# A gated mixer on one core: first block of w_in loaded in one piece, gate row third on ScalarE's queue, second half of block 0 used early

## The chip, the cores and the metric

One core of one Trainium2 chip. The metric is the device time of one execution in microseconds (us), the median over several executions, with the kernel before run in the same rounds. The text quotes means, ranges and the number of runs. All runs used for a comparison are fast, those without a lower clock and a longer time than their like. TensorE does not always get its full clock: in these traces it starts at half clock, at which equal matmuls start twice as far apart (107 against 56 ns for 128 columns), and goes to full clock some us later (at 3.54 to 9.90 us in the profiles below).

## The reference

The program mixes two branches of one input x (2048 rows of 512) with a gate per row:

```python
g = sigmoid((x * gate_w).sum(-1, keepdims=True))
a = A(x)     # linear attention, 32 heads of 16, softmax feature maps, then @ wo
b = B(x):    # z = gelu(x @ w_in), w_in is 512 x 1376
             # z1 = z[:, :688];  z2 = layernorm(z[:, 688:])
             # (z1 * (w_sp @ z2 + b_sp)) @ w_out
out = g * a + (1 - g) * b
```

All inputs are bf16. The change touches only the beginning of `x @ w_in[:, 688:]`: the second half of w_in, four blocks of 128 rows ("block 0" to "block 3"), multiplied with the first two tiles of x. The gate logits x @ gate_w ride along as a 689th column of the same weights.

## The kernel before: the parts that matter

The start of the kernel. HF is 344, FH is 688, P is 128, NDT is 4.

```python
    nc.gpsimd.dma_start(out=gaterow[0:NDT, :], in_=gate_w.rearrange("(dt p) -> dt p", p=P))
    ...
    nc.sync.dma_start(out=xs[:, 0, :], in_=x2[0:P, :])                             # x tile 0
    nc.scalar.dma_start(out=w_z2[:, 0, 0:HF], in_=w_in_v[:, 0, FH:FH + HF])        # block 0, first half
    nc.sync.dma_start(out=xs[:, 1, :], in_=x2[P:2 * P, :])                         # x tile 1
    load_z2w(nc.scalar, 1)                                                         # block 1
    load_z2w(nc.sync, 2)                                                           # block 2
    nc.scalar.dma_start(out=w_z2[:, 0, HF:FH], in_=w_in_v[:, 0, FH + HF:F])        # block 0, second half
    load_z2w(nc.sync, 3)                                                           # block 3
```

TensorE's program for the first two tiles. `one(tt, dt, j)` multiplies tile tt with block dt, columns of half j; `z_part` does a piece of the second half; `warm_up` multiplies constants, to keep TensorE busy until data arrive, and its result is thrown away; `x_T` transposes x through TensorE and copies it out of PSUM (VectorE or ScalarE); `gate_T` turns the gate row into four weight columns.

```python
        warm_up(6)                    # 6 matmuls of 512 columns
        warm_up(2, P)                 # 2 of 128 columns
        x_T(0, 0, 1, ...)             # needs x tile 0
        x_T(0, 1, NDT, ...)
        warm_up(3, P)
        one(0, 0, 0)                  # needs block 0, first half
        x_T(1, 0, 2, ...)
        x_T(1, 2, NDT, ...)
        one(0, 1, 0)                  # needs block 1
        warm_up(1, P)
        one(1, 0, 0)                  # needs the copy of x_T(1, ...)
        one(1, 1, 0)
        for tt in range(2):
            z_part(tt, 1, 0, HF, True)
        gate_T()
        for tt in range(2):
            z_part(tt, 0, 0, HF, False)   # needs block 0, second half
        one(0, 2, 0)
        ...
        for tt in range(2):
            one(tt, 3, 0)             # "row block 3 begins"
            one(tt, 3, 1)
            z2_out(tt, zps[tt])       # the first gelu on ScalarE
```

After that TensorE goes through the other tiles and the attention branch without a pause.

The softmax here doesn't subtract the row's maximum and nothing guards it: scores larger than these inputs give would overflow.

Of the kernel before, what the change touches and what calls it, by code (L numbers as in the profile page):

```python
# [14 lines left out]
P = 128  # L15
# [4 lines left out]
F = 1376  # L20
FH = 688
HF = FH // 2
NT = S // P
NDT = D // P
# [11 lines left out]
def kernel(  # L36
# [14 lines left out]
    nc = tc.nc  # L51
# [10 lines left out]
    xT = pers.tile([P, NDT, S], BF16, name="xT")  # L62
    w_z1 = early.tile([P, NDT, FH], BF16, name="w_z1")
    w_z2 = early.tile([P, NDT, WP], BF16, name="w_z2")
# [27 lines left out]
    gaterow = early.tile([P, P], BF16, name="gaterow")  # L92
# [3 lines left out]
    w_in_v = B_w_in.rearrange("(dt p) f -> p dt f", p=P)  # L96
# [7 lines left out]
        out=ramp[:, 0, :], data0=ones32[:, :], data1=zeros[:, :], initial=0.0,  # L104
# [4 lines left out]
    for q in range(4):  # L109
        qs = slice(32 * q, 32 * q + 32)  # L110
        nc.vector.tensor_tensor(
            out=ident[qs, qs], in0=ramp[qs, 0, :], in1=ramp[qs, 1, :], op=ALU.is_equal)
    nc.gpsimd.dma_start(out=gaterow[0:NDT, :], in_=gate_w.rearrange("(dt p) -> dt p", p=P))
    nc.gpsimd.memset(brow[:], 0.0)
    nc.gpsimd.memset(wphi[:], 0.0)
    def load_z2w(eng, dt):
        eng.dma_start(out=w_z2[:, dt, 0:FH], in_=w_in_v[:, dt, FH:F])  # L117

    nc.sync.dma_start(out=xs[:, 0, :], in_=x2[0:P, :])
    nc.scalar.dma_start(out=w_z2[:, 0, 0:HF], in_=w_in_v[:, 0, FH:FH + HF])  # L120
    nc.sync.dma_start(out=xs[:, 1, :], in_=x2[P:2 * P, :])
    load_z2w(nc.scalar, 1)
    load_z2w(nc.sync, 2)
    nc.scalar.dma_start(out=w_z2[:, 0, HF:FH], in_=w_in_v[:, 0, FH + HF:F])
    load_z2w(nc.sync, 3)
    scrap = early.tile([P, 1], BF16, name="scrap")
    nc.scalar.activation(
        out=scrap[:, :], in_=nc.const_aps.tensor(1.0, [P, 1], BF16), func=AF.Gelu_apprx_tanh)
# [5 lines left out]
    for h in range(2):  # L134
        nc.sync.dma_start(
            out=w_z1[:, 2 * h:2 * h + 2, :], in_=w_in_v[:, 2 * h:2 * h + 2, 0:FH])
    for i in range(4, 8):
        x_dma_T(i)
    for q in range(2, NCH):
        nc.sync.dma_start_transpose(  # L140
            out=xT[:, :, q * CH:(q + 1) * CH], in_=x2[q * CH:(q + 1) * CH, :]
        )
    nc.sync.dma_start(out=brow[0:NT, :], in_=B_b_sp.rearrange("(t p) -> t p", p=P))
    for qk in (1, 0):
        nc.sync.dma_start_transpose(
            out=wqkT[:, qk * NDT:(qk + 1) * NDT, :], in_=A_wqkv[:, qk * D:(qk + 1) * D])
# [4 lines left out]
    for h in range(2):  # L151
        nc.sync.dma_start(
            out=wv_sb[:, 2 * h:2 * h + 2, :],
            in_=A_wqkv[h * 2 * P:(h + 1) * 2 * P, 2 * D:3 * D].rearrange("(dt p) n -> p dt n", p=P),
        )
    for q in range(NCH):
        nc.sync.dma_start_transpose(
            out=wspT[:, :, q * CH:(q + 1) * CH], in_=B_w_sp[q * CH:(q + 1) * CH, :]
# [4 lines left out]
        out=mask4[:], in_=mask4[:], pattern=[[-32, NG]],  # L163
# [3 lines left out]
        out=mask4[:], in_=mask4[:], pattern=[[32, NG]],  # L167
# [3 lines left out]
        out=mask64[:, :, :], in_=mask4[:, :, None].to_broadcast([P, NG, DH]))  # L171
# [7 lines left out]
    def next_turn(kind, n):  # L179
        turn[kind] += 1  # L180
        return f"{kind}{(turn[kind] - 1) % n}"

    def zp_tile():
        return psA.tile([P, 2, CH], FP32, name="zp", tag=next_turn("zp", 3))

    def pq_tile(shape, dtype=FP32):
        return psF.tile(shape, dtype, name="pq", tag=next_turn("pq", 2))

    def z_one(zp, tt, wt, w, dt, j, first=0):
        n = HF if j == 0 else w - HF  # L190
        nc.tensor.matmul(  # L191
            zp[:, j, 0:n], lhsT=xT[:, dt, tt * P:(tt + 1) * P],
            rhs=wt[:, dt, j * HF:j * HF + n],
            start=(dt == first), stop=(dt == NDT - 1), skip_group_check=first > 0,
        )

    def z_mm(tt, wt, w):
        zp = zp_tile()
        for dt in range(NDT):
            for j in range(2):  # L200
                z_one(zp, tt, wt, w, dt, j)
        return zp

    def z2_out(tt, zp):
        z2v = z2all[:, tt, :].rearrange("p (j n) -> p j n", j=2)
        nc.scalar.activation(out=z2v, in_=zp[:, :, 0:HF], func=AF.Gelu_apprx_tanh)  # L206
        nc.vector.tensor_copy(out=glog[:, tt:tt + 1], in_=zp[:, 1, HF:HF + 1])
        for j in range(2):
            nc.vector.bn_stats(out=bn6[:, tt, j, :], in_=z2v[:, j, :])  # L209
        nc.vector.bn_aggr(out=mv[:, tt, :], in_=bn6[:, tt, :, :].rearrange("p j s -> p (j s)"))  # L210
# [4 lines left out]
    def z2_first_two():  # L215
        zps = [zp_tile() for _ in range(2)]
        tp1 = psA.tile([P, 2, P], BF16, name="tp1", tag=next_turn("zp", 3))
        turn["zp"] -= 1

        def warm_up(n, w=CH):  # L220
            for _ in range(n):
                nc.tensor.matmul(
                    zps[0][:, 1, 0:w], lhsT=nc.const_aps.tensor(1.0, [P, P], BF16),
                    rhs=nc.const_aps.tensor(1.0, [P, w], BF16), start=True, stop=True)

        def one(tt, dt, j):
            z_one(zps[tt], tt, w_z2, FH + 1, dt, j, first=j)

        def z_part(tt, dt, c0, c1, start):
            nc.tensor.matmul(  # L230
                zps[tt][:, 1, c0:c1], lhsT=xT[:, dt, tt * P:(tt + 1) * P],
                rhs=w_z2[:, dt, HF + c0:HF + c1], start=start, stop=False, skip_group_check=True)

        warm_up(6)
        warm_up(2, P)
        x_T(0, 0, 1, pq_tile([P, 1, P], BF16)[:, :, :])
        x_T(0, 1, NDT, pq_tile([P, 3, P], BF16)[:, :, :])
        warm_up(3, P)
        one(0, 0, 0)
        x_T(1, 0, 2, tp1[:, :, :])  # L240
        x_T(1, 2, NDT, pq_tile([P, 2, P], BF16)[:, :, :], on_act=True)
        one(0, 1, 0)
        warm_up(1, P)
        one(1, 0, 0)
        one(1, 1, 0)
        for tt in range(2):
            z_part(tt, 1, 0, HF, True)
        gate_T()
        for tt in range(2):
            z_part(tt, 0, 0, HF, False)  # L250
        one(0, 2, 0)
        one(1, 2, 0)
        for tt in range(2):
            one(tt, 2, 1)
            for dt in range(2):
                z_part(tt, dt, HF, HF + 1, False)
        for tt in range(2):
            one(tt, 3, 0)
            one(tt, 3, 1)
            z2_out(tt, zps[tt])  # L260
# [21 lines left out]
    def x_T(i, d0, d1, tp, on_act=False):  # L282
        for dt in range(d0, d1):
            nc.tensor.transpose(tp[:, dt - d0, :], xs[:, i, dt * P:(dt + 1) * P], ident[:, :])
        dst = xT[:, d0:d1, i * P:(i + 1) * P]
        if on_act:
            nc.scalar.copy(out=dst, in_=tp)
        else:
            with tc.high_priority():
                nc.vector.tensor_copy(out=dst, in_=tp)  # L290

    def gate_T():
        gt = pq_tile([P, NDT])
        nc.tensor.matmul(gt[:, :], lhsT=gaterow[:, :], rhs=ident[:, 0:NDT], start=True, stop=True)
        nc.vector.tensor_copy(out=w_z2[:, :, FH], in_=gt[:, :])
# [27 lines left out]
    with tc.manual_schedule(engines={mybir.EngineType.PE, mybir.EngineType.Activation}):  # L323
        z2_first_two()
        z2_tile(2)
        z2_tile(3)
        for c in range(NCH):
            ts = list(range(c * 4, c * 4 + 4))
            for tt in ts:
                if c > 0:  # L330
                    z2_tile(tt)
                if c >= 2 and tt % 4 == 1:
                    later = fold(3 - c)
            for tt in ts:
                z1_tile(tt)
                if c >= 2 and tt % 2 == 0:
                    later.pop(0)()
            z2_norm(ts)
            if c == 1:
                b_T()  # L340
                turn["zp"] += 1
# [274 lines left out]
```

## Time and profile before

| | before |
|---|---|
| median of 3 runs | 207.61 us (207.48 to 207.85) |
| the profiled run | 206.92 us, span 205.2 us |
| TensorE busy | 200.5 us, 98% |
| x tile 0 landed / first transposes | 3.25 / 3.56 us |
| late half of block 0 landed | 5.69 us |
| row block 3 begins / first gelu | 6.71 / 7.20 us |

The timeline of TensorE, columns: start, duration, engine, line, operation, output and inputs, shapes, count.

```profile
...
2.93 0.79 PE L222 MATMUL zp<-const-bfloat16-1.0 128*128 128x512 bf16 x3
3.56 0.39 PE L284 MATMUL pq<-ident,xs 128*128 128x128 bf16 x4
...
4.10 0.32 PE L191 MATMUL zp<-w_z,xT 128*128 128x344 bf16 x1
...
4.48 0.31 PE L191 MATMUL zp<-w_z,xT 128*128 128x344 bf16 x1
4.63 0.22 PE L222 MATMUL zp<-const-bfloat16-1.0 128*128 128x128 bf16 x1
4.92 0.47 PE L191 MATMUL zp<-w_z,xT 128*128 128x344 bf16 x2
5.22 0.46 PE L230 MATMUL zp<-w_z,xT 128*128 128x344 bf16 x2
5.51 0.17 PE L294 MATMUL pq<-ident,gaterow 128*128 128x4 bf16 x1
5.73 0.45 PE L230 MATMUL zp<-w_z,xT 128*128 128x344 bf16 x2
6.02 0.60 PE L191 MATMUL zp<-w_z,xT 128*128 128x344 bf16 x3
...
6.71 2.06 PE L191 MATMUL zp<-w_z,xT 128*128 128x344 bf16 x13
```

L222 are warm-ups, L284 transposes of x, L191 and L230 the weight matmuls, L294 the gate. The trace gives a 344-column matmul 309 ns, but dense ones start every 145 ns, so the starts are what to compare. The holes are before 4.92 (the copy of x tile 1) and before 5.73 (the late half of block 0).

ScalarE's first gelu, our marker of the end of this stage, and what ended the wait for it:

```profile
...
7.20 2.21 ACT L206 ACTIVATE z2all<-zp 128x688 bf16<-128x688 f32 x3 [2.14 <-PE zp L191]
...
```

The loads of the first 1.8 us with the median time from issue to landing:

```profile
...
xs<-in_A_x_dram SPq DMA_DIRECT2D x2, 128.0 KB, 2.5
w_z<-in_B_w_in_dram ACTq DMA_DIRECT2D x2, 86.0 KB, 3.3
...
gaterow<-in_gate_w_dram POOLq DMA_DIRECT2D x1, 1.0 KB, 3.8
```

The 3.3 us of the two halves of block 0 is a median of two very different loads: the first half, issued first on ScalarE's queue at 0.82 us, landed at 3.42 us; the second half, issued third at 1.75 us, at 5.69 us.

### The profile page before, as it was taken

The page shows a single profiled execution, that of the slowest core. Times are in us where ns is not written, and L with a number is a line of the kernel's source. Part 1 is how long each engine was busy: PE and PEld are TensorE (multiplying, and loading weights), DVE is VectorE, ACT ScalarE, POOL GpSimd, SP SyncE. Part 2 cuts the span into 40 slices and gives each one's busy share as a digit, 9 for nine tenths or more (in the row PEclk, how much of TensorE's full clock was granted, in tenths as well). Part 3 has the DMA queues.
Part 4 walks back from the last instruction along what each step waited for, and adds up shares of the span by engine and source line. Part 5 has one row for each costly group of instructions (what it writes and reads, how often), then busy time and mean ns, then how long its engine had stood idle before and what let it go on. Part 6 is the DMA issues. An engine that isn't in the chain of part 4 may idle for free.

```text
span 205.2 us, 3940 instructions
## 1 busy us (share of the span) xinstructions
PE 200.5 (98%) x1522; PEld 119.9 (58%) x1540; DVE 128.5 (63%) x276; ACT 75.6 (37%) x123; POOL 45.3 (22%) x73
## 2 busy tenths in 40 slices
PE   8999999999999999999999999999999999999994
PEld 4666666655665555656565666555455555665642
DVE  4467484837977597979797689555466663633330
ACT  3466678796222333342424042222351126002322
POOL 5020202021523325424242422222204220200000
PEclk9999999999999999999999999999999999999999
DMA  6998699999998027941343229763557467353542
GB/s 190 240 180 186 101 155 246 207 290 230 239 271 188 3 38 193 274 94 24 67 29 64 51 38 135 138 115 75 114 134 80 92 109 183 63 103 67 130 92 77
DMA packets 90099, 27.22 MB, mean 133 GB/s; under 512 B 84224, under 2 KB 90080, under 8 KB 90080
## 3 DMA queue, kind: packets, MB, share of 16 engines
q1 hardware_dynamic: 87312, 24.55, 63.8%
q10 hardware_dynamic: 2736, 2.42, 3.7%
q8 instruction: 12, 0.20, 0.4%
q14 instruction: 7, 0.06, 0.1%
q0 software_dynamic: 32, 0.00, 0.0%
HBM read 4.15 MB, written 2.10 MB: 30 GB/s over the span
## 4 chain that ended last, share of the span: by engine, by line
PE 95%; DMA 2%; issue 1%; ACTq 0%; DVE 0%
PE mm L454 36%; PE zp L191 18%; PE mm L359 13%; PE mm L496 8%; PE mm L399 7%; PE mm L490 7%; PE at L467 2%; PE kvacc L415 2%; DMA w_z<-in_B_w_in_dram 2%; PE mm L500 1%; PE zp L311 0%; PE pq L311 0%; PE zp L230 0%; ACTq L117 0%; ACTq L120 0%
## 5 line engine op out<-in xcount | busy, mean ns | idle before, releaser
L454 PE MATMUL mm<-z2all,wspT 128*128 128x344 bf16 x512 | 79.9, 309 | 0.0
L454 PEld LDWEIGHTS <-wspT 128*128 128x128 bf16 x512 | 49.0, 98 | 25.7 <-issue 0.4
L191 PE MATMUL zp<-w_z,xT 128*128 128x344 bf16 x252 | 37.9, 309 | 0.1
L363 ACT ACTIVATE eq<-mm 128x512 bf16<-128x512 f32 x32 | 17.4, 594 | 51.3 <-PE mm L359 25.6
L367 DVE TENSOR_REDUCE zs<-eq 128x64 f32<-128x1024 bf16 x16 | 19.5, 1220 | 20.4 <-ACT eq L363 20.4
L191 PEld LDWEIGHTS <-xT 128*128 128x128 bf16 x252 | 24.2, 98 | 12.1 <-DVE xT L290 0.5
L459 DVE SCALAR_TENSOR_TENSOR ucat<-mm,bT,z1all 128x344 bf16<-128x344 f32 x32 | 17.4, 544 | 21.9 <-PE mm L454 21.9
L376 POOL TENSOR_TENSOR eq<-eq,ratio 128x512 bf16<-128x512 bf16 x16 | 16.9, 1054 | 50.0 <-DVE ratio L375 41.8
L363 ACT ACTIVATE ek<-mm 128x512 bf16<-128x512 f32 x32 | 17.3, 600 | 27.1 <-PE mm L359 27.1
L511 ACT ACTIVATE ob<-mm,g_inv 128x512 bf16<-128x512 f32 (+1 forms) x16 | 10.9, 681 | 32.8 <-PE mm L500 26.9
L367 DVE TENSOR_REDUCE zs<-ek 128x64 f32<-128x1024 bf16 x16 | 19.3, 1209 | 2.8 <-ACT ek L363 2.8
L496 PE MATMUL mm<-wspT,uT 128*128 128x512 bf16 (+2 forms) x85 | 20.1, 367 | 0.0
L359 PEld LDWEIGHTS <-xT 128*128 128x128 bf16 x128 | 12.2, 98 | 12.9 <-PE mm L500 0.8
L376 POOL TENSOR_TENSOR ek<-ek,ratio 128x512 bf16<-128x512 bf16 x16 | 16.9, 1056 | 2.1 <-DVE ratio L375 1.5
L359 PE MATMUL mm<-wq_p,xT 128*128 128x512 bf16 x55 | 16.0, 379 | 0.5
L399 PE MATMUL mm<-wv_sb,xT 128*128 128x512 bf16 x64 | 16.4, 379 | 0.0
L359 PE MATMUL mm<-wk_p,xT 128*128 128x512 bf16 x61 | 16.1, 379 | 0.2
L490 PE MATMUL mm<-wspT,oT 128*128 128x512 bf16 (+2 forms) x62 | 15.6, 365 | 0.3
L209 DVE BATCH_NORM_STATS2 bn<-z2all 128x6 f32<-128x344 bf16 x32 | 14.9, 502 | 0.0
L206 ACT ACTIVATE z2all<-zp 128x688 bf16<-128x688 f32 x16 | 11.8, 744 | 7.4 <-PE zp L191 7.3
L264 ACT ACTIVATE z1all<-zp 128x688 bf16<-128x688 f32 x16 | 11.9, 744 | 5.1 <-PE zp L191 4.6
L496 PEld LDWEIGHTS <-uT 128*128 128x128 bf16 x85 | 8.1, 98 | 9.4 <-issue 0.2
(74 smaller groups left out, 142.5 us busy)
## 6 DMA issues: line engine op xcount, KB each, us to landing
out_dram<-ob ACTq DMA_DIRECT2D x15, 128.0 KB, 1.7
wspT<-in_B_w_out_dram SPq DMA_DIRECT2D x2, 640.0 KB, 4.9
w_z<-in_B_w_in_dram SPq DMA_DIRECT2D x2, 344.0 KB, 5.0
wv_sb<-in_A_wqkv_dram SPq DMA_DIRECT2D x2, 256.0 KB, 3.7
wspT<-in_A_wo_dram SPq DMA_DIRECT2D x2, 256.0 KB, 4.0
w_z<-in_B_w_in_dram SPq DMA_DIRECT2D x2, 172.0 KB, 3.6
xs<-in_A_x_dram SPq DMA_DIRECT2D x2, 128.0 KB, 2.5
uT<-ucat SPq DMA_TRANSPOSE x16, 2.8
```

Of the source, the lines that this page charges most:

```text
L191: nc.tensor.matmul(zp[:, j, 0:n], lhsT=xT[:, dt, tt * P:(tt + 1) * P], rhs=wt[:, dt, j * HF:j * HF + n], start=(dt == first), stop=(dt == ...
L209: nc.vector.bn_stats(out=bn6[:, tt, j, :], in_=z2v[:, j, :])
L264: nc.scalar.activation(out=z1all[:, tt, :].rearrange("p (j n) -> p j n", j=2), in_=zp[:, :, 0:HF], func=AF.Gelu_apprx_tanh,)
L359: nc.tensor.matmul(ps[:, :], lhsT=xT[:, dt, tt * P:(tt + 1) * P], rhs=w[:, dt, :], start=(dt == 0), stop=(dt == NDT - 1))
L363: nc.scalar.activation(out=e[:, :, a, :], in_=ps[:, :].rearrange("p (h f) -> p h f", f=DH), func=AF.Exp, scale=1.0 - 2.0 * a)
L367: nc.vector.tensor_reduce(out=z[:].rearrange("p h a -> p (h a)"), in_=e[:].rearrange("p h a f -> p (h a) f"), axis=AX.X, op=ALU.add,)
L376: nc.gpsimd.tensor_tensor(out=e[:, :, 1, :], in0=e[:, :, 1, :], in1=ratio[:, :, None].to_broadcast([P, H, DH]), op=ALU.mult)
L399: nc.tensor.matmul(v_ps[:, :], lhsT=xT[:, dt, tt * P:(tt + 1) * P], rhs=wv_sb[:, dt, :], start=(dt == 0), stop=(dt == NDT - 1))
L454: nc.tensor.matmul(gp[:, 0:HF], lhsT=wspT[:, st, tt * P:(tt + 1) * P], rhs=z2all[:, st, j * HF:(j + 1) * HF], start=(st == 0), stop=(st == ...
L459: nc.vector.scalar_tensor_tensor(out=ucat[tt % NU][:, c0 + j * HF:c0 + (j + 1) * HF], in0=gp[:, 0:HF], scalar=bT[:, tt:tt + 1], in1=z1all[ ...
L490: nc.tensor.matmul(acc, lhsT=oTs[tt][:, g, :], rhs=wo_t[:, g, c0:c1], start=start and g == 0, stop=stop and g == NG - 1)
L496: nc.tensor.matmul(acc, lhsT=uTs[tt][:, i + ft, :], rhs=w_main[i][:, ft, c0:c1], start=start and ft == 0, stop=False)
```

## The change

Its intent: block 0 arrives whole, so that the second half can be used early, in the hole before 4.92 us, and nothing large is third on ScalarE's queue; the gate row takes that place and leaves GpSimd's queue. One warm-up and two of four one-column matmuls go.

```diff
-    nc.gpsimd.dma_start(out=gaterow[0:NDT, :], in_=gate_w.rearrange("(dt p) -> dt p", p=P))
...
-    nc.scalar.dma_start(out=w_z2[:, 0, 0:HF], in_=w_in_v[:, 0, FH:FH + HF])
+    load_z2w(nc.scalar, 0)
...
-    nc.scalar.dma_start(out=w_z2[:, 0, HF:FH], in_=w_in_v[:, 0, FH + HF:F])
+    nc.scalar.dma_start(out=gaterow[0:NDT, :], in_=gate_w.rearrange("(dt p) -> dt p", p=P))
...
         one(0, 1, 0)
-        warm_up(1, P)
+        z_part(0, 0, HF, True)
+        gate_T()
         one(1, 0, 0)
         one(1, 1, 0)
+        z_part(1, 0, HF, True)
         for tt in range(2):
-            z_part(tt, 1, 0, HF, True)
-        gate_T()
+            one(tt, 1, 1)
         for tt in range(2):
-            z_part(tt, 0, 0, HF, False)
-        one(0, 2, 0)
-        one(1, 2, 0)
-        for tt in range(2):
+            one(tt, 2, 0)
             one(tt, 2, 1)
-            for dt in range(2):
-                z_part(tt, dt, HF, HF + 1, False)
+            z_part(tt, HF, HF + 1, False)
```

(`z_part` loses its block argument, and `z_one` its `first`; the rest of the kernel is untouched.)

More of the change, by code (lines that the diff above doesn't have):

```diff
@@ L187, in pq_tile, with z_one @@
         return psF.tile(shape, dtype, name="pq", tag=next_turn("pq", 2))
-    def z_one(zp, tt, wt, w, dt, j, first=0):
+    def z_one(zp, tt, wt, w, dt, j, skip=False):
         n = HF if j == 0 else w - HF
@@ L193, in z_one @@
             rhs=wt[:, dt, j * HF:j * HF + n],
-            start=(dt == first), stop=(dt == NDT - 1), skip_group_check=first > 0,
+            start=(dt == 0), stop=(dt == NDT - 1), skip_group_check=skip,
         )
@@ L226, in one, with z_part @@
         def one(tt, dt, j):
-            z_one(zps[tt], tt, w_z2, FH + 1, dt, j, first=j)
-        def z_part(tt, dt, c0, c1, start):
+            z_one(zps[tt], tt, w_z2, FH + 1, dt, j, skip=True)
+        def z_part(tt, c0, c1, start):
             nc.tensor.matmul(
-                zps[tt][:, 1, c0:c1], lhsT=xT[:, dt, tt * P:(tt + 1) * P],
-                rhs=w_z2[:, dt, HF + c0:HF + c1], start=start, stop=False, skip_group_check=True)
+                zps[tt][:, 1, c0:c1], lhsT=xT[:, 0, tt * P:(tt + 1) * P],
+                rhs=w_z2[:, 0, HF + c0:HF + c1], start=start, stop=False, skip_group_check=True)
         warm_up(6)
```

## The prediction

The sum: 4.92 plus nine times 0.145 plus two small is about 6.28 us, 0.42 us under 6.71, and with up to 0.1 us taken back 0.3 to 0.42 us. That TensorE runs in order is seen in before's trace: it waited to 5.73 us for the late half of block 0, although block 2, needed by the matmul after the two of that half, had landed at 5.30.

> **What bounds it now.** TensorE. The page's busy table gives PE 200.5 of 205.2 us (98%); in the chain of waits PE is 95% and the only DMA piece is one load of w_in, 1.75 to 5.69 us (1.9%). That piece is the second half of block 0, issued third on ScalarE's queue. From 5.73 us on the chain is TensorE alone, a 344-column matmul every 145 ns. So the change can only move the moment at which the dense stream begins; nothing after it can get shorter.
>
> **The start of before (timeline, 4.1 to 6.71 us, time at which the row-block-3 matmuls of the first two tiles begin).** TensorE starts one(0,0,0) at 4.10 and one(0,1,0) at 4.48, does a 128-column warm-up (4.63), waits to 4.92 for VectorE's xT copy of tile 1, runs four matmuls, then the gate transpose at 5.51, and waits to 5.73 for the second half of block 0 (landed 5.69). Then five wide matmuls and four 1-column ones; row block 3 begins at 6.71.
>
> **Removed.** One warm-up; two of four 1-column matmuls (25 to 28 ns each); the 0.18 us wait for the late half. **Moved.** z_part(0) of block 0 and the gate transpose go into the hole before 4.92 that waits for xT anyway (4.63 to 4.88), which is where most of the gain comes from. The gate row leaves GpSimd's queue (issued 1.42, landed 5.22) for ScalarE's. **Added.** No arithmetic; the same bytes.
>
> New order: 4.92 (xT of tile 1, unchanged) plus nine wide matmuls at 145 ns plus two small = row block 3 at about 6.28 instead of 6.71: 0.42 us saved.
>
> **Do the loads arrive?** Block 0's first half landed at 3.42, block 1 at 4.18. [...] Block 0's rows are now 8 packets of 1376 B per engine instead of 8 of 688 B: by the trace's DMA records 59 against 34 ns, so 0.2 us later. Estimates: whole block 0 at 3.6 (needed 4.10), block 1 at 4.4 (needed 4.48, harmless to about 4.55), gate row right behind it at 4.5 to 4.7 (harmless to about 4.85), x rows 0.1 later, which the warm-ups hide. Block 2 (5.30) and block 3 (5.91) should come no later, being needed at 5.65 and 6.28. The gate column is cast by 5.2, used at 5.37.
>
> **What takes some back.** Being 0.4 us earlier, TensorE nearly meets xT of tiles 2 and 3 (landed 6.84, now needed 6.87) and the second half of the z1 weights (landed 9.80, now needed 9.79): up to 0.1 us. Later loads have more slack.
>
> **Prediction.** 0.3 to 0.42 us gained: 207.25 us; 8 in 10 between 206.9 and 207.65. Faster by over 2%: 0.01; within 2%: 0.98; slower by over 2%: 0.01.
>
> **What would show it.** Timeline: one wide matmul and the gate transpose before 4.92, no wait on a weight load, row block 3 at about 6.3, first gelu output 0.4 us earlier than 7.20. DMA landings: block 0 under 4.1, gate row under 4.85. Chain: the w_in piece shrinks or is replaced by the x load and its transposes.
>
> **What would make it wrong.** TensorE runs in order, so a late gate row stalls everything behind it: landing at 5.3 would cancel the gain. Block 1 after 4.6, or x rows after 3.6, would shift all. A wait at the z1 weights could take back more than 0.1 us. Repeat spread before is 0.37 us, as large as the effect.

## More of the kernel before

Lines of the page: the span, TensorE's busy time, two rows of 40 slices in tenths (TensorE's busy share and its granted clock), and the chain of waits by engine and by line.

```profile
span 205.2 us, 3940 instructions
...
PE 200.5 (98%) x1522; PEld 119.9 (58%) x1540; DVE 128.5 (63%) x276; ACT 75.6 (37%) x123; POOL 45.3 (22%) x73
...
PE   8999999999999999999999999999999999999994
...
PEclk9999999999999999999999999999999999999999
...
PE 95%; DMA 2%; issue 1%; ACTq 0%; DVE 0%
PE mm L454 36%; PE zp L191 18%; PE mm L359 13%; PE mm L496 8%; PE mm L399 7%; PE mm L490 7%; PE at L467 2%; PE kvacc L415 2%; DMA w_z<-in_B_w_in_dram 2%; PE mm L500 1%; PE zp L311 0%; PE pq L311 0%; PE zp L230 0%; ACTq L117 0%; ACTq L120 0%
...
```

TensorE works for 95% of the chain, and one load of w_in ("DMA w_z", 2%) is nearly all that the chain has before TensorE's stream. The PEclk row says full clock from the first slice on. That is not so, as we shall see: the trace's clock record begins only at 3.54 us in this run, and a slice without a record shows as full.

## The result

| | before | after |
|---|---|---|
| median, 6 runs each | 207.46 us (206.92 to 207.85) | 207.32 us (206.93 to 207.73) |
| ratio, 95% interval | | 0.9996 (0.9978 to 1.0015) |
| span of the profiled run | 205.2 us | 205.6 us |
| TensorE at full clock from | 3.54 us | 6.02 us |
| x tile 0 landed / first transposes | 3.25 / 3.56 us | 3.75 / 3.80 us |
| block 0 complete / block 1 landed | 5.69 / 4.18 us | 3.94 / 4.68 us |
| row block 3 begins / first gelu | 6.71 / 7.20 us | 7.30 / 7.79 us |

Ratios here and below are the mean time of one kernel's fast runs over that of the other's fast runs of the same rounds, so not quite the ratio of the medians quoted. Some of the ratios (experiments 4, 8 and 12) leave the profiled run out, so they can differ a little from the means quoted beside them, which use all fast runs. The means differ by 0.08 us, which is within the noise; 0.3 to 0.42 us were forecast. And the profile is not the one that was forecast. The first gelu is 0.59 us later, not 0.4 us earlier.

Lines of the page after:

```profile
span 205.6 us, 3949 instructions
...
PEclk9999999999999999999999999999999999999999
...
PE 98%; DVE 0%; issue 0%
PE mm L450 36%; PE zp L190 18%; PE mm L355 14%; PE mm L492 8%; PE mm L486 7%; PE mm L395 7%; PE at L463 2%; PE kvacc L411 2%; PE zp L221 2%; PE mm L496 1%; PE pq L280 0%; PE zp L307 0%; PE zp L229 0%; PE pq L307 0%; DVE ob L503 0%; PE tp L2
...
```

The load of w_in has gone from the chain, which is TensorE for 98% now. The PEclk row still shows full clock everywhere.

The timeline of TensorE after:

```profile
...
2.92 0.85 PE L221 MATMUL zp<-const-bfloat16-1.0 128*128 128x512 bf16 x3
3.80 0.61 PE L280 MATMUL pq<-ident,xs 128*128 128x128 bf16 x4
...
4.52 0.49 PE L190 MATMUL zp<-w_z,xT 128*128 128x344 bf16 x1
...
5.23 0.49 PE L190 MATMUL zp<-w_z,xT 128*128 128x344 bf16 x1
5.52 0.49 PE L229 MATMUL zp<-w_z,xT 128*128 128x344 bf16 x1
5.81 0.21 PE L290 MATMUL pq<-ident,gaterow 128*128 128x4 bf16 x1
5.88 0.51 PE L190 MATMUL zp<-w_z,xT 128*128 128x344 bf16 x2
...
7.30 1.48 PE L190 MATMUL zp<-w_z,xT 128*128 128x344 bf16 x9
```

The order is the wanted one: a wide matmul at 5.52 and the gate transpose at 5.81 stand in the former hole, nothing waits for a weight load. But every step takes twice as long. The transposes take 0.61 us for four instead of 0.39; the trace has them 107 ns apart instead of 56; the wide matmul at 5.23 is followed after 0.29 us instead of 0.15. TensorE is at half clock until 6.02 us here, and was at full clock from 3.54 us in the profile of before.

The first gelu, the loads and the only wait of TensorE's weight loads for a transfer between 3 and 11 us:

```profile
...
7.79 2.21 ACT L205 ACTIVATE z2all<-zp 128x688 bf16<-128x688 f32 x3 [1.94 <-PE zp L190]
...
```

```profile
...
w_z<-in_B_w_in_dram ACTq DMA_DIRECT2D x2, 172.0 KB, 3.3
xs<-in_A_x_dram SPq DMA_DIRECT2D x2, 128.0 KB, 3.1
...
gaterow<-in_gate_w_dram ACTq DMA_DIRECT2D x1, 1.0 KB
```

```profile
...
PEld L280 <- DMA xs<-in_A_x_dram: 0.3, 1, 0.3
```

The x rows now take 3.1 us to land instead of 2.5, and TensorE waits 0.3 us for them.

So there are two theories of where the 0.36 us (half-way between the 0.3 and 0.42 us forecast) went:

- **Clock.** The moment of TensorE's full clock differs from execution to execution (3.54 us in one profile, 6.02 us in the other). The profile of before caught an early one, and the forecast gain came from holes that exist only then. At half clock (287 ns from one wide matmul to the next instead of 145) TensorE would come to the loads only when they have landed.
- **Loads.** The whole rows of block 0 (1376 B instead of 688 B) move beside the x rows and delay them by 0.5 us (3.25 to 3.75 us), whatever the clock.

### The profile page after: what moved, and what is told of

It reads as the page before. It is cut to its first block, busy times and chain, and to the rows that moved or that the text cites. A ratio compares the mean times of both kernels' runs of the same rounds, so it can differ in the third digit from the quotient of the medians.

```text
span 205.6 us, 3949 instructions
## 1 busy us (share of the span) xinstructions
PE 202.0 (98%) x1537; PEld 120.4 (59%) x1537; DVE 128.6 (63%) x276; ACT 75.4 (37%) x123; POOL 44.5 (22%) x72
## 4 chain that ended last, share of the span: by engine, by line
PE 98%; DVE 0%; issue 0%
PE mm L450 36%; PE zp L190 18%; PE mm L355 14%; PE mm L492 8%; PE mm L486 7%; PE mm L395 7%; PE at L463 2%; PE kvacc L411 2%; PE zp L221 2%; PE mm L496 1%; PE pq L280 0%; PE zp L307 0%; PE zp L229 0%; PE pq L307 0%; DVE ob L503 0%; PE tp L280 0%
## 5 line engine op out<-in xcount | busy, mean ns | idle before, releaser
L190 PE MATMUL zp<-w_z,xT 128*128 128x344 bf16 (+1 forms) x254 | 38.6, 311 | 0.0
L486 PE MATMUL mm<-wspT,oT 128*128 128x512 bf16 (+2 forms) x68 | 16.6, 366 | 0.0
```

Of the source, the lines that this page charges most:

```text
L190: nc.tensor.matmul(zp[:, j, 0:n], lhsT=xT[:, dt, tt * P:(tt + 1) * P], rhs=wt[:, dt, j * HF:j * HF + n], start=(dt == 0), stop=(dt == NDT ...
L486: nc.tensor.matmul(acc, lhsT=oTs[tt][:, g, :], rhs=wo_t[:, g, c0:c1], start=start and g == 0, stop=stop and g == NG - 1)
```

## The experiments

Twelve runs, one repeat each of before and of after among them, all with five rounds beside before. All gave the reference's result.

**1. Before, unchanged.** No edit.

> The kernel before, unchanged. CLOCK theory (the moment at which TensorE goes from 107 to 56 ns per 128-column matmul varies from execution to execution by up to about 3 us, and the profile of before caught an early one, 3.54 us): ratio 1.000 within 0.002; times spread over about 0.9 us as before; in this profile the step can lie anywhere between about 3 and 6.2 us, and if it is later than 3.54 the row-block-3 matmuls begin later than 6.71 us, by up to 0.8 us. LOADS theory (the change itself delays the x rows by 0.5 us and so delays everything): here xs lands at 3.25 and 3.89 us as in the first profile, within 0.1 us, whatever the clock does.

Measured: median 207.30 us (206.86 to 207.76, 6 runs), ratio 1.0000 (0.9984 to 1.0016). TensorE's timeline in its profiled run, which took 207.76 us:

```profile
...
3.57 0.63 PE L284 MATMUL pq<-ident,xs 128*128 128x128 bf16 x4
...
4.32 0.49 PE L191 MATMUL zp<-w_z,xT 128*128 128x344 bf16 x1
...
6.57 0.21 PE L294 MATMUL pq<-ident,gaterow 128*128 128x4 bf16 x1
6.66 0.52 PE L230 MATMUL zp<-w_z,xT 128*128 128x344 bf16 x2
...
7.70 1.18 PE L191 MATMUL zp<-w_z,xT 128*128 128x344 bf16 x7
```

The x rows landed at 3.32 and 4.16 us, the first transposes started at 3.57, as in the first profile. But half clock lasted until about 6.8 us (read from the spacing of the matmuls: the last at 287 ns begins at 6.28, the first at 147 ns after 6.87), 3.3 us longer than in the first profile and past the 3 to 6.2 us expected, and row block 3 begins at 7.70 us, 0.99 us later than in the first profile of the same kernel. The late half of block 0 landed at 6.62 us here, and TensorE came to it at 6.66 us: almost no hole. The clock theory's number ("by up to 0.8 us") was slightly exceeded. One kernel, two executions, 205.2 and 206.0 us of span: the start explains it, for from the first matmul of the next stage (k) to the end both take 161.3 us, as do all profiles of the fast state below (161.26 to 161.43).

**2. After, unchanged.**

> The changed kernel, unchanged. CLOCK theory: if the step comes early (about 3.5 us) the row-block-3 matmuls begin at 6.3 to 6.5 us; if late (about 6 us) at 7.3 us as in the first profile of after; mean ratio to before 0.998 to 0.9995 (the order fills a hole only in executions with an early step). LOADS theory: xs lands at about 3.75 and 4.45 us again, whatever the clock does, and TensorE's first transposes start at 3.80 and not at 3.56; ratio 1.000.

Measured: median 206.95 us (206.63 to 207.44, 6 runs), mean 0.35 us under before's of the same rounds, ratio 0.9985 (0.9968 to 1.0002). Full clock from 5.97 us, first gelu 7.79 us, the same picture as the first profile; x rows landed at 3.80 and 4.50 us, transposes at 3.85. Both theories have what they asked for: the x rows are late again, and the clock was late again. With the first result's 0.08 us, the mean gain over 12 runs is 0.22 us, with an uncertainty (two standard errors, from a spread of 0.3 us per run) of about as much, so it is not separated from zero.

**3. The load alone.** Before's TensorE order and GpSimd gate row, block 0 in one piece:

```diff
-    nc.scalar.dma_start(out=w_z2[:, 0, 0:HF], in_=w_in_v[:, 0, FH:FH + HF])
+    load_z2w(nc.scalar, 0)
...
-    nc.scalar.dma_start(out=w_z2[:, 0, HF:FH], in_=w_in_v[:, 0, FH + HF:F])
```

> Kernel before with block 0 of w_in loaded in one piece first on ScalarE's queue, nothing third; TensorE's order and the gate row's queue as before. LOADS theory: xs lands at 3.75 and 4.45 us, first transposes at 3.8 us, time 0.1 to 0.3 us over before when the clock steps early. CLOCK theory: xs lands within 0.15 us of its landing in before's repeat; the wait at 5.69 is gone, so with an early step row block 3 begins at about 6.55 instead of 6.71; ratio 0.9990 to 1.0000.

Measured: x rows at 3.73 and 4.40 us, transposes at 3.78; ratio 1.0002 (0.9985 to 1.0019).

```profile
...
xs<-in_A_x_dram SPq DMA_DIRECT2D x2, 128.0 KB, 3.0
...
```

The clock theory's guess for the x rows (within 0.15 us) is refuted, that of the loads theory holds: the one piece delays x, without anything else of the change. The time does not show it. Full clock came at 6.78 us in this profile, so its first gelu (8.27 us) compares with the 8.19 us of experiment 1, whose clock came at about the same time.

**4. The gate row back on GpSimd's queue**, the rest as after.

```diff
-    nc.scalar.dma_start(out=gaterow[0:NDT, :], in_=gate_w.rearrange("(dt p) -> dt p", p=P))
+    nc.gpsimd.dma_start(out=gaterow[0:NDT, :], in_=gate_w.rearrange("(dt p) -> dt p", p=P))
```

> Changed kernel with the gate row back on GpSimd's queue. If the gate row lands at 5.2 us as in before: with an early clock step the gate transpose, now ahead of everything, waits to about 5.25 and row block 3 begins about 0.35 us later than in the changed kernel with the same step; with a late step (TensorE reaches the gate transpose at 5.8 us) no wait at all. Mean time over the changed kernel by 0 to 0.35 us, 0.1 likely.

Measured: mean 207.47 us against 207.00 us of the changed kernel in the same rounds, 0.47 us more (two standard errors 0.35; against all twelve runs of the changed kernel 0.30 us), ratio to before 1.0012 (0.9997 to 1.0028). The profiled run had an early clock, 4.09 us, and the gate row landed at 5.19 us:

```profile
...
PEld L290 <- DMA gaterow<-in_gate_w_dram: 0.4, 1, 0.4
...
```

```profile
...
7.13 2.21 ACT L205 ACTIVATE z2all<-zp 128x688 bf16<-128x688 f32 x3 [1.86 <-PE zp L190]
...
```

So the move of the gate row to ScalarE's queue is a necessary part: with the new order the gate transpose stands in front of everything, and on the old queue it would hold TensorE up. In this run first gelu came at 7.13 us in spite of a clock 0.55 us later than before's 7.20 us: with an early clock the new order gains, as far as two profiles can show it.

**5 to 7. The clock taken out, first try (failed).** A GpSimd memset of 8256 elements held back the first loads while TensorE did 28 warm-ups, so that the loads would meet a TensorE already at full clock. The same was done to after, and to after with block 0 in two pieces.

```diff
+    nc.gpsimd.memset(z1all[:, 0:12, :], 1.0)
+    nc.gpsimd.tensor_copy(out=w_z2[:, 0, 0:1], in_=z1all[:, 0, 0:1])   # the same for xs, go, gaterow
...
-        warm_up(6)
+        warm_up(28)
+        warm_up(12, lhsT=go[:, :])
```

> Kernel before with its whole start pushed back about 9 us, so that TensorE has its full clock before the first load is issued: GpSimd's 8256-element memset holds back all first loads, TensorE does 28 warm-up matmuls meanwhile and 12 once the memset is over. CLOCK theory: the spread of this kernel's times falls from 0.9 us to under 0.4 us, every 128-column matmul after the hold takes 56 ns spacing, and the start looks like the first profile of before: from the first xs issue to row block 3 about 5.9 us. If the clock is not the cause of the spread, the spread stays at 0.9 us.

> The changed kernel with the same hold. The clock being out of it, what is left is the loads. LOADS theory (the whole block delays the x rows by 0.45 us, TensorE starts its transposes 0.25 us later, and the hole that the change fills is 0.42 us): 0.15 to 0.25 us faster than before with the hold. If the x rows' delay did not matter: 0.42 us faster. If the change is worth nothing: 0.0.

> The changed kernel with the hold, but block 0 in two half pieces issued first and second on ScalarE's queue, then block 1, then the gate row: same bytes in the same order, in 688-byte rows. LOADS theory, in the form 'the size of the rows in the other queue delays the x rows': x rows land within 0.1 us of before's, transposes 0.25 us earlier than in the changed kernel with the hold; block 1 lands 0.2 to 0.3 us later than there, which costs up to 0.2 us back; net 0.0 to 0.2 us faster than the changed kernel with the hold. In the rival form 'the bytes ahead delay the x rows, whatever the rows' size': x rows land as late as in the changed kernel, net 0.0 to 0.2 us slower.

Measured: 219.50, 219.62 and 219.28 us. The hold did not do what it should: the compiler's scheduler moved the other loads of SyncE ahead of the held x rows, which landed at 15.1 us, and TensorE idled 3.8 us. No conclusion about the change is drawn. But the clock can be seen to fall in the windows view of the first of the three (columns: stretch, length, then busy time and count for PE, PEld, DVE, ACT, POOL, then the granted clock, DMA share, GB/s):

```profile
...
4.00:14.00 10.00, 7.36 (x35) 3.17 (x33) 0.00 (x0) 0.00 (x0) 6.87 (x17) 1.00 1.21 234
14.00:20.80 6.80, 5.61 (x32) 3.56 (x33) 1.05 (x4) 0.37 (x1) 0.00 (x0) 0.50 0.97 195
20.80:30.00 9.20, 9.20 (x64) 6.16 (x63) 5.79 (x20) 6.46 (x9) 1.28 (x2) 1.00 0.64 123
...
```

Here the clock column shows half clock (0.50 from 14.00 to 20.80 us), for now it lies inside the record: the clock fell while TensorE idled, from 11.36 to 15.19 us. The record's full and half stretches are 10.24 and 6.83 us long here (and the half one 3.41 us in the third kernel); in before and in after the full one is 201.39 us. What sets these lengths, no run shows.

Nor does any run show what decides the moment of full clock. TensorE's first warm-up starts at 0.84 to 0.85 us in the first profiles of before and of after, and the warm-ups are the same (six of 512 columns, 427 ns apart), yet full clock came at 3.54 us in one and at 6.02 us in the other. What is measured is the range: in the profiles of the table below in which no wait of TensorE after its warm-ups passed 0.4 us, full clock came between 3.54 and about 6.8 us; in the two with waits of 1 us (experiments 10 and 11, below) at 9.90 and 9.24 us. The profile on which the prediction stood had the earliest of all nine.

**8 and 9. The clock taken out, second try.** Same idea, a longer memset (11008 elements), 30 and 11 warm-ups, and the queues' order kept by force.

```diff
+    with tc.manual_schedule(engines={SP, Activation, Pool}):   # names cut
+        nc.gpsimd.memset(z1all[:, :, :], 1.0)
+        ...                                    # the copies, then all first loads in the kernel's order
-        warm_up(6)
+        warm_up(30)
+        warm_up(11, lhsT=go[:, :])
```

> Kernel before held back about 10 us again, now with the order of every queue kept (in the first try the x load had slipped behind others, so TensorE idled 4 us and lost its clock). CLOCK theory: no 107 ns spacing after the hold, and the spread of the times falls from 0.9 us to under 0.4 us; x rows land about 2.45 us after their issue and row block 3 begins about 5.9 us after it, as in the first profile of before. If the clock's moment is not the cause of the spread, it stays at 0.9 us.

> The changed kernel with the same hold. LOADS theory (whole rows in the other queue delay the x rows by about 0.45 us, of which TensorE feels 0.25 us; the new order is worth 0.42 us): 0.15 to 0.25 us faster than before with the hold, x rows landing 2.9 us after issue. If the x rows' delay did not matter: 0.42 us faster. If the change is worth nothing at full clock: 0.0.

Measured: before 216.68 to 217.44 us (5 runs, mean 217.11), after 216.21 to 216.76 us (4 fast runs, mean 216.40). At full clock the change gains 0.71 us (two standard errors 0.38), more than either number expected. Part of this may be the hold's own doing: it pushed GpSimd's queue back further than the others, so that in before's profile the gate row (15.44 us) came after the late half of block 0 (15.33 us), and TensorE, which could have gone on at 15.37 us, did so at 15.60. Up to 0.23 us of the gain can come from that, in that profile. In before's profile there is full clock throughout from 4.38 us on, and the x rows landed 2.25 us after their issue; row block 3 begins 6.05 us after the first issue against 5.90 in the first profile of before. The expectation that before's spread would fall under 0.4 us failed: it is 0.76 us, with a granted clock of 1.0 in all five. The clock is therefore not the only cause of the spread. The load that came third on ScalarE's queue is the suspect: it landed at 5.69 us in one profile of before and at 6.62 in the other (SyncE's third load, issued beside it, at 5.30 and 6.12, so it is not this queue alone), and in after, which has no such load, three of four runs lie within 0.11 us. No profile shows the slow ones of before, so this is argued, not shown.

After's fifth run, the profiled one, was slow (what limited its clock, nothing shows) and is left out:

```profile
...
core 0: 366.5 us, clock 0.561
...
```

Its x loads can still be read, for they were issued at 10.5 and 11.0 us as in before's: x rows 2.58 and 3.24 us after their issue against 2.25 and 2.82 us in before's, so the delay is there with the hold too, 0.3 to 0.4 us. (Before's profile was at full clock; this one was not, so at full clock on both sides the delay is not shown.)

**10. Small rows, same bytes.** After, with block 0 in two pieces, one after the other.

```diff
-    load_z2w(nc.scalar, 0)
+    for j in range(2):
+        nc.scalar.dma_start(out=w_z2[:, 0, j * HF:(j + 1) * HF], in_=w_in_v[:, 0, FH + j * HF:FH + (j + 1) * HF])
```

> The changed kernel, no hold, block 0 in two half pieces issued one after the other (half, half, block 1, gate row): same bytes, same order, rows of 688 B. LOADS theory in the form 'rows of the other queue, by size': x rows land at 3.3 and 3.9 to 4.2 us as in before, first transposes at 3.56, block 1 lands near 4.9. Rival form 'bytes ahead': x rows at 3.75 and 4.45 us as in the changed kernel. Time 0.1 to 0.3 us under the changed kernel in the first form, equal in the second; the clock's spread hides much of it.

Measured: 208.05 us (207.85 to 209.82), ratio 1.0055 (1.0022 to 1.0087), slower. The loads theory's first form holds: x rows at 3.23 and 3.82 us, transposes at 3.56. (A rival is left: the two pieces are issued 0.45 us apart, so at first a smaller load, and not only one of smaller rows, stands beside the x rows.)

```profile
...
xs<-in_A_x_dram SPq DMA_DIRECT2D x2, 128.0 KB, 2.5
...
w_z<-in_B_w_in_dram ACTq DMA_DIRECT2D x1, 172.0 KB, 4.5
```

But block 1, now third on ScalarE's queue, took 4.5 us and landed at 6.24 us, not near 4.9; SyncE's third load, issued beside it, took 4.34 us. TensorE waited for it (starts; the bracket is the idle time and what ended it):

```profile
...
3.56 0.63 PE L281 MATMUL pq<-ident,xs 128*128 128x128 bf16 x4
...
6.28 0.45 PE L191 MATMUL zp<-w_z,xT 128*128 128x344 bf16 x1 [1.05 <-DMA w_z<-in_B_w_in_dram]
...
```

And the wait seems to have cost more than itself. Full clock came only at 9.90 us, against about 6.8 us in experiment 1, which had no such wait: half clock lasted about 3.1 us longer, which costs up to half of that in TensorE's work (an estimate from the spacing of equal matmuls, 287 against 147 ns). That the wait put full clock off is argued from this profile and that of experiment 11, not shown. The six runs fall into two groups, 207.85 to 208.11 us (four) and 209.72 to 209.82 us (two), whose means are 1.81 us apart.

**11. x rows split over both queues ahead of all, one warm-up less**, with the two pieces of experiment 10.

```diff
-    nc.sync.dma_start(out=xs[:, 0, :], in_=x2[0:P, :])
+    nc.sync.dma_start(out=xs[0:64, 0, :], in_=x2[0:64, :])
+    nc.scalar.dma_start(out=xs[64:P, 0, :], in_=x2[64:P, :])
...
-        warm_up(6)
+        warm_up(5)
```

> Try at a better version: the halves as in the run beside it, and the first x tile split over both hardware queues ahead of everything, with one warm-up of 512 columns less so that TensorE is ready for it. LOADS theory with the CLOCK theory: in most executions TensorE is still at half clock, so the start is TensorE work from the first transposes on; x lands at 2.7 to 2.9 us, transposes start at 3.0 to 3.1 instead of 3.56 (before) and 3.80 (changed): 0.4 to 0.6 us faster than before on average, ratio 0.997 to 0.998. If loads of w_in then come last (block 0 after 3.6, block 1 after 4.6 us), 0.2 us.

Measured: 209.61 us, ratio 1.0123 (1.0081 to 1.0165), the worst of all, a clear miss. One half of x tile 0 landed only at 3.45 us, x tile 1 at 5.33, block 1 at 6.28; TensorE waited for each of the three, and full clock came at 9.24 us. Four loads ahead of the gate row on ScalarE's queue did not bring anything in earlier.

**12. Both x tiles first, nothing large third.** After, with two loads exchanged:

```diff
-    load_z2w(nc.scalar, 0)
-    nc.sync.dma_start(out=xs[:, 1, :], in_=x2[P:2 * P, :])
+    nc.scalar.dma_start(out=xs[:, 1, :], in_=x2[P:2 * P, :])
+    load_z2w(nc.sync, 0)
```

> Changed kernel with two loads exchanged between the queues: the second x tile first on ScalarE's queue, block 0 of w_in second on SyncE's; so both x tiles go ahead of every weight row, with no third large load on ScalarE's queue. LOADS theory (whole weight rows moving beside them delay the x rows by 0.45 us and TensorE's first transposes by 0.25 us): x rows land at 3.0 to 3.3 us both, transposes at 3.56 (end of the warm-ups) instead of 3.80, block 0 at 3.9 to 4.1 and block 1 at 4.2 to 4.6 us; no wait of TensorE over 0.2 us in an execution whose clock steps at 5 us or later; time 0.15 to 0.3 us under the changed kernel, ratio to before 0.997 to 0.9985. Rival (the x rows' delay does not matter for the time): ratio as the changed kernel's two runs, 0.9985 to 0.9996.

Measured: 207.37 us (207.02 to 207.65, 5 runs), mean 0.22 us under before's of its rounds, ratio 0.9986 (0.9973 to 1.0000). The x rows landed at 3.40 and 3.57 us, later than the 3.0 to 3.3 expected. The transposes start at 3.57 us as expected, but block 0 landed at 4.48, so the first weight matmul begins where it does in after (4.52 us):

```profile
...
3.57 0.63 PE L280 MATMUL pq<-ident,xs 128*128 128x128 bf16 x4
...
4.52 0.45 PE L190 MATMUL zp<-w_z,xT 128*128 128x344 bf16 x1
...
```

The delay has moved from the x rows to the weights. The ratio is the same as after's own two, so it is not shown to beat after, and the rival expectation (the x rows' delay does not matter for the time) is not refuted.

The profiled runs together (landing times and the clock are from the trace's records; experiments 1 and 12 have no clock record, the moment is read from the matmuls' spacing; 5 to 9, whose start is held back, are left out):

| run | full clock from | first transposes | first weight matmul | first gelu | span |
|---|---|---|---|---|---|
| before | 3.54 | 3.56 | 4.10 | 7.20 | 205.2 |
| before again (1) | about 6.8 | 3.57 | 4.32 | 8.19 | 206.0 |
| after | 6.02 | 3.80 | 4.52 | 7.79 | 205.6 |
| after again (2) | 5.97 | 3.85 | 4.57 | 7.79 | 205.6 |
| block 0 whole (3) | 6.78 | 3.78 | 4.50 | 8.27 | 206.2 |
| gate row on GpSimd (4) | 4.09 | 3.66 | 4.27 | 7.13 | 205.3 |
| two pieces (10) | 9.90 | 3.56 | 4.31 | 10.18 | 208.1 |
| x split over both queues (11) | 9.24 | 3.59 | 4.29 | 9.89 | 207.9 |
| both x tiles first (12) | about 6.75 | 3.57 | 4.52 | 8.12 | 205.9 |

The first gelu follows the clock more than the kernel. An estimate from these rows: TensorE has no hole in after from 3.80 us on, so a clock 0.75 us later than its 6.02 us would cost it half of that, 0.38 us, and bring its gelu to 8.17 us; before has 8.19 us with that clock. By this estimate the change is worth nothing with a late clock. With an early one, experiment 4 came first although its clock was later and its gate row held it up.

## Why the prediction was right or wrong

- **The time: right, but by luck.** 207.32 us against 207.25, inside the range, and within 2%. But the range also holds 207.61 us, the median of before that was then known, so no gain at all would have fitted; and before's own median fell to 207.46 us with three more runs. The gain between the means was 0.08 us, not 0.3 to 0.42.
- **"From 5.73 us on the chain is TensorE alone … nothing after it can get shorter": right.** From the first k matmul on, every profile but the slow one takes 161.3 us. Also right: an earlier start gives a little back. The way from the first gelu to the first k matmul is 36.55 us in the profiles with a late clock, 36.68 us in before's and 36.81 us in experiment 4.
- **"New order: 4.92 … row block 3 at about 6.28 instead of 6.71: 0.42 us saved": not so in other executions.** This is the step that failed. It took the one profiled execution of before, which was the fastest of its kernel's first six, for the typical one; of the 54 runs of before, 4 took 206.92 us or less. The hole before 4.92 us and the wait to 5.73 us are those of a TensorE at full clock from 3.54 us, the earliest of the nine profiles. In the other profile of before the clock came at about 6.8 us, TensorE reached the late half of block 0 at 6.66 us when it had just landed, and there was no hole to fill. The gain is a mixture: about nothing with a late clock (estimate above), 0.71 us when the clock is held at full (experiments 8 and 9, up to 0.23 us of it perhaps the hold's), and 0.22 us on average over 12 runs, which the noise does not separate from zero. That it is a mixture is argued: no run shows the clock's moment and the time of many executions together.
- **"x rows 0.1 later, which the warm-ups hide": wrong in size.** They were 0.5 us later (3.25 to 3.75 and 3.89 to 4.46), and TensorE's first transposes 0.24 us later. Experiments 3 and 10 show what does it: the one-piece load alone delays them, two pieces with the same bytes do not. The first x tile landed at 3.23 to 3.32 us where the other queue's first rows have 688 B (before, 1, 10), at 3.40 with 1024 B (12) and at 3.62 to 3.80 with 1376 B (after, 2, 3, 4); whether the row or the whole first load counts, these runs do not separate. The estimate counted 59 instead of 34 ns per row of the other queue. The trace's DMA records show that the loss lies at the very start: of the 256 x rows, 65 and 61 had started by 2.4 us in the two profiles of before and 59 in experiment 10, but 24 and 36 in the two of after and 38 in experiment 3. In after's first profile single x rows took up to 736 ns there, but in its repeat none over 320, and the x rows were as late; so slow single reads are not the whole of it. Nor had ScalarE's rows taken their place: of these too, only 2, 7 and 4 had started by 2.4 us in the two profiles of after and experiment 3, against 25, 24 and 17 in before's two and experiment 10. Why the larger load slows the start of both queues stays open. Whether the delay costs time stays open too: experiment 12 removed most of it and the wait came back at block 0.
- **"Block 0 at 3.6, block 1 at 4.4, gate row in time": right in kind, 0.3 us early.** 3.94 and 4.68 us. No wait followed. How the engines take turns between the queues no run here shows; that the rows ahead can be counted one by one was the author's estimate. The runs show only that the size of one queue's loads changes when the other's land (x tile 0 at 3.25 us beside 688 B rows, at 3.75 us beside 1376 B rows).
- **"Landing at 5.3 would cancel the gain": right.** Experiment 4 did just that (5.19 us; TensorE waited 0.4 us for it), and its mean was not under before's.
- **"Repeat spread before is 0.37 us": too small.** Over six runs it was 0.93 us, and its causes, as far as argued here, are the clock's moment and the late landing of the third loads. It differs between the experiments: the nine runs of before beside experiment 12 lie within 0.26 us (207.48 to 207.74), which is not explained.

## What to carry to other kernels

Compare the profiled run with the timed ones before costing anything in its first microseconds: here a profile of a lucky execution showed holes that another execution of the same kernel did not have. Read TensorE's clock from the spacing of equal matmuls (107 against 56 ns for 128 columns here), not from a row of averages, and look twice at a hole before the first full-clock moment: in the two profiles with waits of 1 us there, full clock came at 9.24 and 9.90 us, in the other seven by about 6.8 us. When a load is made larger to save an issue, look at what is loaded beside it: what it delays may be the first thing that the kernel needs (x tile 0, from 3.25 to 3.75 us here). And do not cost the third 128-row load of a queue like the second: on ScalarE's queue it landed 3.94, 4.87 and 4.5 us after its issue in three profiles (before, 1, 10), against 2.9 and 3.1 us for the second in the first two; SyncE's third, issued beside it, took 3.56, 4.38 and 4.34 us.
